# Attention and expert routing on one core: where in the pipeline the load of a pair's values is issued

## The chip, the cores and the metric

The kernel runs on one core of one Trainium2 chip. The time is the device time of one execution in microseconds (us), lower is better. The runs of the kernel before the change took 830.01, 833.48 and 834.38 us, so the median is 833.48 us. Engines are named as in the profile: PE is TensorE's matmul row and PEld its weight loads, DVE is VectorE, ACT is ScalarE, POOL is GpSimd, SP is SyncE, and SPq is SP's sequencer, which here issues DMAs.

## What is computed

Eight batches of eight heads are put through causal attention with a decay bias, and the result goes through a layer of eight experts that takes one expert per token.

```
B, H, S, D = 8, 8, 576, 64
scores = q @ k.T / sqrt(D)
cum = cumsum(max(s, 0), -1)
scores = where(causal, -1e9, scores + min(-(cum_i - cum_j), 0))
attn = softmax(scores)
x = (attn @ v).transpose(0, 2, 1, 3).reshape(B * S, H * D)

logits = x @ w_gate + modality_bias[modality_id]
e = argmax(logits); gate = softmax(logits)[e]
out = gate * (relu(x @ w1[e]) @ w2[e])
```

## The kernel before

**Two halves.** The first, class `Attn`, does the attention in 32 pairs. A pair is one head of two batches, 576 positions each. The second half takes the tokens, sorted by expert, in blocks of 256 rows and multiplies them with w1 and w2. The change touches the first half alone.

**A pair.** Queries and keys come as raw tiles, `rawq` and `rawk`, and are split for float precision into a high part (`QH`, `KA`) and a low part. POOL does the splitting in `prep` (L312 to L342): two copies rawk to KA (L322), two copies rawq to QH (L322), two subtractions into QL and two into KA (L326). Between them SP copies KA's upper rows into another tile, KB (L332), which also gets the rows of the decay bias (L249, L250, in the first pairs L262 and L281). PE multiplies KA with QH (L372) and KB with QL (L394) into a score, DVE adds the mask and finds the row maximum (L396), ACT takes the exponential (L416), PE turns the result over (L433, L448), ACT and DVE copy it to `PT`. Then PE multiplies it with the pair's values, tile `V` (L474): first 20 matmuls for the later queries, and some steps later 8 for the earlier ones. The 20 and the 8 of a pair are the marks by which the text counts pairs. Pair 0 has its 20 at 23.62 us of the profiled execution, pair 1 at 34.85, and pair 31 at 376.59.

**The steps.** `run` (L501) walks through 32 x 9 steps k. A pair has nine steps, one for each of the nine pieces of its score. The transposes run three steps behind the scores, and the products with V some steps behind those, so the 20 matmuls of a pair fall into the first steps of the next pair. During a pair's steps `prep` prepares the queries and keys of the next pair, and loads are written into the program for later pairs: V in the sixth step (L520), for the next pair, and rawq and rawk in the eighth (L522), for the pair after the next.

**What sets the order.** The program is written in that order, and a scheduler decides at build time how each engine's instructions stand, by readiness in its own reckoning and by the order in which they are written. It also sets the semaphores. SP issues its DMAs strictly in that order: one that must wait holds up all behind it. The tiles `V`, `rawq` and `rawk` come from the pool `ld` with two buffers each (L298, L308), so the load of the V of pair p+2 may not start before the 8 matmuls of pair p have read theirs.

Of the kernel before, what the change touches and what calls it, by code (L numbers as in the profile page):

```python
# [38 lines left out]
class Attn:  # L39
# [318 lines left out]
        return after  # L358

    def start(self, pi, x):  # L360
        st = dict(pi=pi, h=pi % 8, x=x, s={}, high={}, PT=self.PT[pi % 2], V=self.V.pop(pi))
        st["mx"] = self.sm.tile([P, 10], F32, name="mx")
        st["sums"] = self.sm.tile([P, 9], F32, name="sums")
        return st
# [136 lines left out]
    def run(self, npair, newx, done, setup):  # L501

        bg = self.bg = []
        seq = [(pi, i) for pi in range(npair) for i in ORDER]
        sts = {}
        prev, prepg, n = [], None, len(seq)
        for k in range(n + LAG + 9):
            if k < n:
                pi, i = seq[k]
                if k % 9 == 0:  # L510
                    sts[pi] = self.start(pi, newx(pi // 8) if pi % 8 == 0 else sts[pi - 1]["x"])
                    prepg = self.prep(pi + 1) if pi + 1 < npair else None
                with self.behind() if pi or not self.pe else self.tc.issue_after(self.pe[-1]):
                    self.score(sts[pi], i)
                if k in setup:
                    with self.newest():
                        more = setup[k]()
                        if more is not None:
                            bg.append([more, False])
                if k % 9 == 5 and 0 < pi < npair - 1:  # L520
                    self.V[pi + 1] = self.load_v(pi + 1)
                if k % 9 == 7 and 0 < pi < npair - 2:  # L522
                    self.raw[pi + 2] = self.load_qk(pi + 2)
                if prepg is not None:
                    next(prepg, 0)
            if prev and next(prev[0][0], 0) == 0:
                _, st, g = prev.pop(0)
                if g == 0 and st["pi"] % 8 == 7:
                    bg.append([done(st["pi"] // 8, st["x"]), False])
            for j in () if k == LAG else (0, 1) if k == LAG + 1 else (k - LAG,) if LAG < k < n + LAG else ():  # L530
                p0, i0 = seq[j]
                with self.behind():
                    self.trans(sts[p0], i0)
                if i0 in (8, ORDER[-1]):
                    g = int(i0 == 8)
                    prev.append((self.tail(sts[p0], g), sts[p0], g))
            if not prev and k >= n + LAG:
                break
            for b in list(bg):
                if k >= b[1] if b[1] > 1 else k % 9 in QUIET or not b[1]:  # L540
                    with self.newest():
                        b[1] = next(b[0], None)
                    if b[1] is None:
                        bg.remove(b)
        assert not prev
        return bg
# [847 lines left out]
```

## Time and profile before

| | us |
|---|---|
| median of three runs | 833.48 |
| fastest, slowest run | 830.01, 834.38 |
| the profiled execution | 832.43 |
| its span in the profile | 830.6 |
| around the span (832.43 - 830.6) | 1.83 |
| attention, to the end of the last product with V | about 381 |
| expert layer | about 449 |

Both halves are bound by PE, which is busy for 98% of the span. A profile row of the timeline gives the start, the duration, the engine, the line of the program, the operation with the tile written and the tiles read, the shape and a count where like instructions follow each other. A bracket at its end is the idle time of the engine ahead of it and what ended it. That releaser is inferred: where the engine named had long been done, it was another, often a DMA.

### The profile page before, as it was taken

To read this page: it belongs to the slowest core of one execution; us is meant where nothing else is said; L and a number is where in the kernel's file an instruction comes from. 1 tells how busy PE (TensorE), PEld (TensorE's weight loads), DVE (VectorE), ACT (ScalarE), POOL (GpSimd) and SP (SyncE) were. 2 spreads that over 40 slices of the span, in tenths; PEclk is the share of its full clock that TensorE was granted. 3 is DMA by queue.
4 is the path that set the end of the run, shared out by engine and by line. 5 is a ranking of instruction groups with operands and counts; after the bars stand their busy time and mean duration, and the time that the engine had idled before them with its cause. 6 is when DMAs were issued, how large, how long until landed. Compare 5 with 4: busy or idle time off the path is not lost. (4 is left out here: it accounts for less than half of the span.)

```text
span 830.6 us, 16652 instructions
## 1 busy us (share of the span) xinstructions
PE 814.3 (98%) x5692; PEld 698.1 (84%) x5692; DVE 539.6 (65%) x1405; ACT 530.5 (64%) x1196; POOL 360.3 (43%) x383
## 2 busy tenths in 40 slices
PE   7989999999999999999999999999999999999996
PEld 6768788788788888888888999998888999988884
DVE  7655676666766677766479865565666655546874
ACT  6867788878888887876365554454455554445663
POOL 8767777998789877993511000000000000000001
PEclk9999999999999999999999999999999999999999
DMA  7574456777567655737598866555556666555970
GB/s 235 157 221 130 159 184 200 226 228 224 153 192 222 218 178 175 243 136 285 200 374 315 312 258 256 206 220 203 209 200 246 257 257 240 207 191 221 373 241 28
DMA packets 68547, 182.29 MB, mean 219 GB/s; under 512 B 7993, under 2 KB 8889, under 8 KB 68334
## 3 DMA queue, kind: packets, MB, share of 16 engines
q1 hardware_dynamic: 62622, 161.17, 57.5%
q0 software_dynamic: 5840, 20.06, 6.2%
q8 instruction: 45, 0.74, 0.4%
q14 instruction: 40, 0.33, 0.1%
HBM read 144.73 MB, written 26.80 MB: 207 GB/s over the span
## 5 line engine op out<-in xcount | busy, mean ns | idle before, releaser
L1075 POOL DMA_INDIRECT out<-ys,oi x36 | 37.0, 1028 | 368.1 <-ACT ys L1074 296.9
L396 DVE CUSTOM_DVE_ANT_0 pe<-sp,mk 128x512 f32<-128x512 f32 (+3 forms) x256 | 122.4, 488 | 106.0 <-PE sp L394 95.1
L416 ACT ACTIVATE pe<-pe,mx 128x512 f32<-128x512 f32 (+3 forms) x256 | 144.3, 565 | 17.8 <-DVE mx L396 15.0
L437 ACT COPY PT<-pt 128x512 f32<-128x512 f32 (+1 forms) x192 | 97.1, 509 | 23.3 <-PE pt L433 23.3
L433 PE MATMUL pt<-ident,pe 128*128 128x128 f32 x640 | 111.2, 280 | 0.3
L372 PE MATMUL sp<-KA,QH 128*128 128x256 f32 (+2 forms) x256 | 102.6, 403 | 5.2 <-POOL KA L326 3.3
L1091 ACT ACTIVATE hT<-hp 128x512 fp32r<-128x512 f32 x72 | 42.8, 595 | 92.5 <-PE hp L1089 91.7
L474 PE MATMUL o<-PT,V 128*64 128x320 f32 (+4 forms) x896 | 101.8, 367 | 0.0
L474 PEld LDWEIGHTS o<-PT,V 128*64 128x64 f32 x896 | 59.1, 137 | 47.7 <-issue 15.8
L1089 PE MATMUL hp<-xT,wcb 128*128 128x256 f32 x648 | 89.6, 282 | 0.0
L1089 PE MATMUL hp<-xT,wca 128*128 128x256 f32 x624 | 87.4, 282 | 0.5 <-ACT xT L1041 0.5
L433 PEld LDWEIGHTS pt<-ident,pe 128*128 128x128 f32 x640 | 76.8, 144 | 12.6 <-issue 5.3
L326 POOL TENSOR_TENSOR KA<-rawk,KA 64x576 fp32r<-64x576 f32 x62 | 86.9, 1418 | 0.2
L394 PE MATMUL sp<-KB,QL 76*128 76x256 f32 (+2 forms) x256 | 85.5, 337 | 1.5 <-DMA QL<-ek 1.5
L326 POOL TENSOR_TENSOR QL<-rawq,QH 64x576 fp32r<-64x576 f32 x62 | 86.6, 1412 | 0.2
L1089 PEld LDWEIGHTS hp<-xT,wcb 128*128 128x128 f32 x648 | 83.1, 188 | 0.6
L1092 DVE SCALAR_TENSOR_TENSOR hT<-hp,hT 128x512 fp32r<-128x512 f32 x72 | 49.5, 687 | 51.6 <-ACT hT L1091 51.6
L1089 PEld LDWEIGHTS hp<-xT,wca 128*128 128x128 f32 x624 | 80.4, 188 | 1.4 <-issue 0.7
L1064 PE MATMUL y<-wcb,hT 128*128 128x512 f32 x336 | 81.2, 398 | 0.0
L1064 PEld LDWEIGHTS y<-wcb,hT 128*128 128x128 f32 x336 | 62.8, 188 | 14.7
L1089 PE MATMUL hp<-xT,wcc 128*128 128x256 f32 x456 | 64.6, 281 | 0.0
L322 POOL TENSOR_SCALAR KA<-rawk 128x576 fp32r<-128x576 f32 x60 | 39.3, 671 | 58.2 <-PE sp L372 25.0
(285 smaller groups left out, 1620.9 us busy)
## 6 DMA issues: line engine op xcount, KB each, us to landing
wrbw<-in_w SPq DMA_DIRECT2D x104, 512.0 KB
wraw<-in_w SPq DMA_DIRECT2D x56, 512.0 KB
rawq<-in_qkv SPq DMA_DIRECT2D x31, 576.0 KB
rawk<-in_qkv SPq DMA_DIRECT2D x31, 576.0 KB
xg<-lists SPq DMA_DIRECT2D x18, 576.0 KB
V<-in_qkv SPq DMA_DIRECT2D x32, 320.0 KB
KB<-KA SPq DMA_DIRECT2D x62, 144.0 KB
lists<-z SPq DMA_DIRECT2D x8, 576.0 KB
```

The source lines that it names most:

```text
L326: self.last = nc.gpsimd.tensor_tensor(o, i, h, ALU.subtract).ins
L372: self.pe.append(self.nc.tensor.matmul(sp[:, :nn], QH[:, q0:q0 + P], self.KA[u][:, ab, :nn], start=True, stop=False).ins)
L394: self.pe.append(nc.tensor.matmul(sp[:, :nn], QL[:EXT, q0:q0 + P], KB[:EXT, ab, :nn], start=False, stop=True).ins)
L396: ins = nc.vector.tensor_tensor_reduce(out=t[:, :n], in0=sp[:, :n], in1=self.mk[:, 512 - n:512], scale=-0.125, scalar=3.0e38, op0=ALU.add, ...
L416: self.act = nc.scalar.activation(t[:, :n], t[:, :n], AF.Exp, bias=m, scale=-1.0, accum_out=st["sums"][:, o:o + 1]).ins
L433: self.pe.append(nc.tensor.transpose(out=pt[:, o:o + P], in_=pe[:, P * j:P * j + P], identity=self.ident).ins)
L437: cp(w[:, :, :, v:v + P], pt[:, :n * (1 + both)].rearrange("p (a j q) -> p a j q", a=1 + both, q=P))
L474: m = nc.tensor.matmul(o[r, f - q0:q1 - q0], V[:, ab, j, :], PT[:, ab, PTS * j + f if j < 4 else PTW - 64:PTS * j + q1 if j < 4 else PTW], ...
L1064: self.last[0] = nc.tensor.matmul(y[u], hT[:, a, f, P * u:P * u + P], W[4 + f // 2][:, c, 512 * (f % 2):512 * (f % 2) + 512], start=f == 0 ...
L1089: nc.tensor.matmul(hp[:, u], W[k][:, a, f:f + P], xT[:, c, k], start=k == 0 and i == 0, stop=k == 3 and i == 2)
L1091: hi = nc.scalar.activation(hs, hp, AF.Relu)
L1092: lo = nc.vector.scalar_tensor_tensor(hT[:, 1, 2 * m:2 * m + 2], hp, 0.0, hs.bitcast(F32), ALU.max, ALU.subtract)
```

## The change

The load of V is written at another step. Before, the sixth step of a pair issued the load for the next pair. Now the third step of a pair issues the load of this same pair. Pairs 0 and 1, whose values are loaded at the start, are as before.

```diff
-        st = dict(pi=pi, ..., V=self.V.pop(pi))
+        st = dict(pi=pi, ..., V=self.V.pop(pi, None))
...
-                if k % 9 == 5 and 0 < pi < npair - 1:
-                    self.V[pi + 1] = self.load_v(pi + 1)
+                if k % 9 == 2 and pi > 1:
+                    sts[pi]["V"] = self.load_v(pi)
```

On PE, DVE and ACT no instruction changes its place. On SP the loads of V move in pairs 2 to 10, at a few places up to pair 16 by one or two rows, and once at the end. On POOL one scatter of the routing (L732) moves behind one subtraction.

The first place is SP in pairs 1 and 2, as one piece of the difference. KB and KA are the key tiles, `mt` small constants of the routing, rawq and rawk the raw tiles of pair 3 above and of pair 4 below.

```order
 L281 DMA QL_103<-ek 2x64 x2
 L332 DMA KB_107<-KA_105 64x576 x2
-L309 DMA V<-in_qkv 128x640
 L304 DMA rawq<-in_qkv 128x1152
 L304 DMA rawk<-in_qkv 128x1152
```

```order
 L332 DMA KB_108<-KA_106 64x576 x2
+L309 DMA V<-in_qkv 128x640
 L638 DMA mt<-in_mid 128x72
 L639 DMA mt<-in_mb 128x16
-L309 DMA V<-in_qkv 128x640
```

In pair 1 a V stood ahead of the raw tiles of pair 3, and none stands there now. In pair 2 a V stands directly behind the KB copies. It is the V of pair 2 now, where before the V of pair 3 stood behind the constants.

The second place is SP in pair 3, and the pairs up to 8 read alike. In brackets are the semaphores that a row waits for: a DMAHW is that of an earlier DMA, Pool and PE are those of the engines. First before the change:

```order
L332 DMA KB_107<-KA_105 64x576 [waits DMAHW5_49,Pool_49]
L332 DMA KB_107<-KA_105 64x576 [waits DMAHW6_49,Pool_49]
L309 DMA V<-in_qkv 128x640 [waits DMAHW7_49,PE_49]
L304 DMA rawq<-in_qkv 128x1152 [waits DMAHW0_49]
L304 DMA rawk<-in_qkv 128x1152 [waits DMAHW1_49]
```

And with the change:

```order
L332 DMA KB_107<-KA_105 64x576 [waits DMAHW4_49,Pool_49]
L332 DMA KB_107<-KA_105 64x576 [waits DMAHW5_49,Pool_49]
L309 DMA V<-in_qkv 128x640 [waits DMAHW6_49]
L304 DMA rawq<-in_qkv 128x1152 [waits DMAHW7_49]
L304 DMA rawk<-in_qkv 128x1152 [waits DMAHW0_49]
```

The rows stand as before, but this V is that of pair 3 and no longer that of pair 4, and it waits for no semaphore of PE: its buffer has been free for a pair.

The third place is SP at the end of the attention, where the load of the V of pair 31 stands between loads of the first weights (`wraw`) of the expert layer.

```order
 L940 DMA wraw<-in_w 128x1024
-L309 DMA V<-in_qkv 128x640
-L940 ISA
-L940 DMA wraw<-in_w 128x1024
+L940 ISA
+L940 DMA wraw<-in_w 128x1024
+L309 DMA V<-in_qkv 128x640
```

V stands behind one more load of weights there. In pairs 11 to 30 the V of the same pair stands at the same place, or one or two rows from it, in both programs, and waits for PE in both.

More of the change, by code (lines that the diff above doesn't have):

```diff
@@ L360, in start @@
     def start(self, pi, x):
-        st = dict(pi=pi, h=pi % 8, x=x, s={}, high={}, PT=self.PT[pi % 2], V=self.V.pop(pi))
+        st = dict(pi=pi, h=pi % 8, x=x, s={}, high={}, PT=self.PT[pi % 2], V=self.V.pop(pi, None))
         st["mx"] = self.sm.tile([P, 10], F32, name="mx")
```

## The prediction

> **What bounds the kernel.** The page's busy times come first:
>
> ```profile
> span 830.6 us, 16652 instructions
> PE 814.3 (98%) x5692; PEld 698.1 (84%) x5692; DVE 539.6 (65%) x1405; ACT 530.5 (64%) x1196; POOL 360.3 (43%) x383
> ```
>
> PE is idle for 830.6 - 814.3 = 16.3 us of the whole span, and the change takes no work from PE. So it can win only where PE waits or runs slowly, and lose only where it makes PE wait. The view by windows and the waits inside one window tell where PE is disturbed (columns: window, length, busy us of PE, PEld, DVE, ACT and POOL with counts, granted clock, DMA share, GB/s):
>
> ```profile
> 50.00:75.00 25.00, 22.65 (x160) 17.51 (x160) 14.45 (x56) 16.76 (x50) 17.69 (x21) 0.93 0.58 194
> 382.00:831.00 449.00, 441.35 (x2825) 396.42 (x2823) 286.92 (x400) 232.09 (x296) 50.48 (x47) 1.00 0.66 241
> ```
>
> ```profile
> PE sp L372 <- POOL KA L326: 2.3, 2, 1.9
> ```
>
> The expert layer has no load of V. From 50 to 75 us PE loses 2.35 us of 25, and nearly all of it (2.3 us in two waits) is for POOL's last preparation step, the subtractions into KA. The granted clock is under 1 there too.
>
> Next I measure each pair's period by its 20 products with V, in the timeline of PE: pairs 1 to 6, then 10, 11 and 12.
>
> ```profile
> 34.85 2.28 PE L474 MATMUL o<-PT,V 128*64 128x320 f32 x20
> 47.17 2.28 PE L474 MATMUL o<-PT,V 128*64 128x320 f32 x20
> 61.70 3.38 PE L474 MATMUL o<-PT,V 128*64 128x320 f32 x20
> 73.97 2.27 PE L474 MATMUL o<-PT,V 128*64 128x320 f32 x20
> 85.58 2.27 PE L474 MATMUL o<-PT,V 128*64 128x320 f32 x20
> 96.73 2.28 PE L474 MATMUL o<-PT,V 128*64 128x320 f32 x20
> ...
> 141.63 2.27 PE L474 MATMUL o<-PT,V 128*64 128x320 f32 x20
> 153.42 2.28 PE L474 MATMUL o<-PT,V 128*64 128x320 f32 x20
> 164.60 2.27 PE L474 MATMUL o<-PT,V 128*64 128x320 f32 x20
> ```
>
> An undisturbed period is 11.15 us (85.58 to 96.73) or 11.18 (153.42 to 164.60), say 11.16. The periods into pairs 2, 3, 4 and 5 are 12.32, 14.53, 12.27 and 11.61, which is 1.16, 3.37, 1.11 and 0.45 too long, and the one into pair 11 is 11.79, 0.63 too long. From 96.73 to 141.63 four pairs take 44.90, 0.26 over, which I leave in place as extra routing work. **What is to be had is 1.16 + 3.37 + 1.11 + 0.45 + 0.63 = 6.72 us.** The largest piece looks so:
>
> ```profile
> 58.94 0.50 PE L372 MATMUL sp<-KA,QH 128*128 128x512 f32 x1 [1.91 <-POOL KA L326]
> 60.31 0.61 PE L372 MATMUL sp<-KA,QH 128*128 128x512 f32 x1 [0.43 <-POOL KA L326]
> ```
>
> ```profile
> 61.00:62.00 1.00, 1.00 (x4) 0.35 (x5) 0.62 (x1) 0.00 (x0) 0.00 (x0) 0.50 0.94 382
> ```
>
> PE waits 1.91 + 0.43 us at the head of pair 4's scores, then the granted clock is 0.50 and the 20 products of pair 3 take 3.38 us where others take 2.28. So a stall costs its length and about 1.1 us of slow clock.
> [...]
>
> **Why POOL is late.** These rows are SP, PE and POOL in pair 1, then in pair 4:
>
> ```profile
> 25.43 1.18 SPq L332 DMA_DIRECT2D KB<-KA  x2
> 29.37 0.87 PE L474 MATMUL o<-PT,V 128*64 128x256 f32 x8
> 30.28 0.33 SPq L309 DMA_DIRECT2D V<-in_qkv  x1
> 31.14 0.42 SPq L304 DMA_DIRECT2D rawk<-in_qkv  x1
> 37.67 1.31 POOL L322 TENSOR_SCALAR KA<-rawk 128x576 fp32r<-128x576 f32 x2 [4.75 <-PE sp L394]
> ...
> 64.21 1.15 SPq L332 DMA_DIRECT2D KB<-KA  x2
> 68.44 0.87 PE L474 MATMUL o<-PT,V 128*64 128x256 f32 x8
> 69.35 0.33 SPq L309 DMA_DIRECT2D V<-in_qkv  x1
> 70.20 0.82 SPq L304 DMA_DIRECT2D rawk<-in_qkv  x1
> 76.12 1.31 POOL L322 TENSOR_SCALAR KA<-rawk 128x576 fp32r<-128x576 f32 x2 [2.96 <-DMA QL<-ek]
> ```
>
> SP is done with the KB copies at 26.61 and 65.36. Then it stands at the load of V, whose buffer PE frees with the 8 products (ending 30.24 and 69.31), and issues V 0.04 us later. The raw tiles queue behind V, and POOL starts 5.1 us after rawk's issue ended in pair 4 (6.1 in pair 1, with large stores behind). POOL's row names other releasers, but the distance to rawk fits every time. Where POOL isn't held by raw tiles, it starts with the first score of the pair, as in pair 29:
>
> ```profile
> 342.25 0.40 PE L372 MATMUL sp<-KA,QH 128*128 128x512 f32 x1
> 342.24 1.32 POOL L322 TENSOR_SCALAR KA<-rawk 128x576 fp32r<-128x576 f32 x2
> ```
>
> That is about 1.5 us before the 20 products, while at 76.12 POOL starts 2.15 us after them (73.97).
>
> **What the change does, part by part.** The number of loads, their bytes and all work on PE, DVE and ACT stay. On SP, in pairs 2 to 10, V is the pair's own, waits for no PE, and the raw tiles behind it are issued 30.28 - 26.61 = 3.7 us (pair 1, where V is also gone from ahead of them: another 0.3) to 69.35 - 65.36 = 4.0 us (pair 4) earlier. I take 4.0.
>
> Pair 3: its preparation moves from 37.67 to about 33.7, its late end goes, 1.16 us. Pair 4, whose preparation is this:
>
> ```profile
> 44.65 1.01 SPq L304 DMA_DIRECT2D rawk<-in_qkv  x1
> 52.20 1.30 POOL L322 TENSOR_SCALAR KA<-rawk 128x576 fp32r<-128x576 f32 x2 [5.99 <-PE sp L407]
> 57.49 2.77 POOL L326 TENSOR_TENSOR KA<-rawk,KA 64x576 fp32r<-64x576 f32 x2
> ```
>
> Here V hardly waited; rawk was late because all of SP had been pushed back in pair 1. With 4.0 us off, the two subtractions end at 54.9 and 56.3 where they ended at 58.9 and 60.3. PE would have come for the first at 58.94 - 1.91 = 57.03, less the 1.16 already won 55.9, and for the second 0.9 us later: no stall, 3.37 us gone, and with the slow clock pair 5's 1.11. Pair 5 is the tightest:
>
> ```profile
> 70.53 1.41 POOL L326 TENSOR_TENSOR KA<-rawk,KA 64x576 fp32r<-64x576 f32 x1
> 73.33 0.48 PE L372 MATMUL sp<-KA,QH 128*128 128x512 f32 x1
> ```
>
> KA is ready at 71.94 for a PE that comes at 73.33, 1.39 us of slack. PE comes 1.16 + 3.37 + 1.11 = 5.64 us earlier, POOL 4.0: a new wait of 5.64 - 4.0 - 1.39 = 0.25 us. From pair 6 on the second saving of 4.0 comes on top, and 0.45 and 0.63 go. **Sum: 6.72 - 0.25 = 6.5 us.** DVE and ACT, at 14.45 and 16.76 us of the 25, have room for it.
>
> Is V now late? Its usual lead is from the end of the KB copies to its 20 products, 65.36 to 73.97: 8.6 us. The tightest is pair 3, whose V follows KB copies delayed by large stores:
>
> ```profile
> 55.54 1.14 SPq L332 DMA_DIRECT2D KB<-KA  x2
> ```
>
> Less 4.0, V is issued at 52.7; the products come at 34.85 + 2 x 11.16 = 57.2, so 4.5 us. The time that a load of V takes alone is in no row. It is bounded by V and both raw tiles, 69.35 to 76.12, 6.8 us, and by zero; nearest is one load of 512 KB against V's 320, in the rows below 367.84 to 371.72, 3.9 us. I take 3.9: no wait. At 6.8 pair 3 alone would wait, 2.3 us, with a slow clock 3.4.
> [...]
>
> At the end V of pair 31 goes behind one more load of weights:
>
> ```profile
> 367.84 0.38 SPq L940 DMA_DIRECT2D wraw<-in_w  x1
> 368.57 0.37 SPq L309 DMA_DIRECT2D V<-in_qkv  x1
> 370.17 0.34 SPq L940 DMA_DIRECT2D wraw<-in_w  x1
> ...
> 371.72 1.05 POOL L963 TENSOR_SCALAR wca<-wraw 128x1024 fp32r<-128x1024 f32 x1 [1.57 <-DMA wraw<-in_w]
> 376.59 2.28 PE L474 MATMUL o<-PT,V 128*64 128x320 f32 x20
> ```
>
> V's issue moves from 368.57 to 370.6, 6.0 us before its use. Taken as 3.9 us it is free; as 6.8 it costs 0.8. I take none. The scatter behind one subtraction comes 1.4 us later and nothing on PE asks for it there. In pairs 11 to 30 V keeps its place behind the same PE wait.
>
> **How the numbers follow.** The profiled execution took 832.43 (span 830.6 and 1.83 around it), 1.05 under the median of 833.48. Less 6.5 this is 825.9 from the one and 827.0 from the other; I predict 826.5. A change by 0.5%, 4.2 us, is about what a measurement of this kernel tells from none.
>
> - Forecast, the stalls go: 826.5, chance 0.62; 824 to 829 by the residue in pair 5 and the runs' own spread.
> - **Half of it.** The raw tiles are earlier, but pair 4's stall stays, because ekd's and eqd's stores around rawk, or constants on POOL, hold the preparation all the same. For it: rawk to POOL took 6.5 us there (45.66 to 52.20), not 5.1. Against: those stores come after rawk in SP's order. 6.5 - 3.4 = 3.1 us remain, 829.8; chance 0.22, a quarter of that beyond 0.5%.
> - **Nothing.** The releasers in POOL's rows are right, POOL waits for PE (L394, L407) and not for rawk, or the scheduler's order makes the change idle. Against: they name another line at each start, none the last reader of that KA. 832.4; chance 0.11.
> - **Slower: V is late in all of pairs 2 to 10.** If a load of V needs more than the 8.6 us, PE waits with its 20 products in nine pairs. At 10.3 us it is 9 x 1.7 = 15.3 us, less 6.5, 841; it turns slower by 0.5% from 8.6 + (6.5 + 4.2) / 9 = 9.8 us. Against: V and two larger tiles together took 6.8. Chance 0.05.
>
> Faster 0.62 + 0.05 = 0.67, less 0.02 for a shallow forecast: 0.65; same 0.30; slower 0.05. The range 823.5 to 831.0 takes in the forecast and its half, 0.84, with a little off at its ends.
>
> **What would show it.** Right: no row of PE waiting for KA in pairs 3 and 4, the 20 products of pair 3 at 2.28 us, periods of 11.2 throughout, pair 12's at about 158 and the granted clock 1.00 from 50 to 75 us; V without a PE wait, the raw tiles directly behind the KB copies, POOL starting some 4 us earlier. Wrong: POOL starting at the old distance from PE's pairs, a DMA wait ahead of the 20 products, or the gain lost again behind 380 us.

## The result and the profile after

The changed kernel took 826.51 us in the median of eight runs, seven of them between 825.16 and 827.06, against 833.37 us for eight runs of the kernel before (830.01 to 835.79). The eighth run took 2291 us, for a reason that its record does not show, and is left out of the ratio. **The ratio is 0.9916, with a 95% interval of 0.9895 to 0.9937**: faster by 0.84%, about 7 us. The profiled execution took 826.59 us.

The page of the changed kernel, its span and PE's busy time:

```profile
span 824.9 us, 16646 instructions
PE 813.0 (99%) x5692; PEld 699.1 (85%) x5692; DVE 540.3 (66%) x1405; ACT 530.5 (64%) x1196; POOL 359.2 (44%) x383
```

PE's idle time fell from 16.3 to 824.9 - 813.0 = 11.9 us. Its 5692 matmuls are the same, and they took 814.3 - 813.0 = 1.3 us less. The view by windows, for the window in which PE was busy for 22.65 of 25 us before:

```profile
50.00:75.00 25.00, 25.00 (x196) 20.59 (x195) 16.60 (x65) 20.00 (x61) 20.87 (x25) 1.00 0.56 176
```

PE is busy without a gap and the granted clock is 1.00. The 20 products of pairs 1 to 5, then of pairs 10 to 12, in the timeline of PE:

```profile
36.12 2.27 PE L474 MATMUL o<-PT,V 128*64 128x320 f32 x20
47.33 2.27 PE L474 MATMUL o<-PT,V 128*64 128x320 f32 x20
58.57 2.27 PE L474 MATMUL o<-PT,V 128*64 128x320 f32 x20
69.72 2.27 PE L474 MATMUL o<-PT,V 128*64 128x320 f32 x20
80.89 2.28 PE L474 MATMUL o<-PT,V 128*64 128x320 f32 x20
...
136.98 2.28 PE L474 MATMUL o<-PT,V 128*64 128x320 f32 x20
148.15 2.27 PE L474 MATMUL o<-PT,V 128*64 128x320 f32 x20
159.31 2.27 PE L474 MATMUL o<-PT,V 128*64 128x320 f32 x20
```

The periods are 11.21, 11.24, 11.15 and 11.17 us where they were 12.32, 14.53, 12.27 and 11.61, and 11.17 into pair 11, where it was 11.79. No 20 products take longer than 2.28. From pair 1 to pair 12 it is 159.31 - 36.12 = 123.19 us and was 164.60 - 34.85 = 129.75: 6.56 us less. The span fell by only 830.6 - 824.9 = 5.7, since pair 0 came at 24.91 and not at 23.62 in this execution. That start varies from trace to trace (23.16 to 25.32 in this study). Up to there both kernels have the same instructions in the same order, and the granted clock of the start differs: it was 0.50 for 3.41 us in the first trace of before and for 10.24 us here. Still, the start came at 23.79 or later in the four traces of kernels in which all nine loads are moved, and at 23.62 or earlier in the other six; whether that is chance is open.

The chain that was held up, in pair 1 and then in pair 4, from SP's and POOL's timelines:

```profile
26.45 1.15 SPq L332 DMA_DIRECT2D KB<-KA  x2
28.28 0.44 SPq L304 DMA_DIRECT2D rawk<-in_qkv  x1
34.29 1.30 POOL L322 TENSOR_SCALAR KA<-rawk 128x576 fp32r<-128x576 f32 x2 [0.83 <-PE sp L372]
...
60.96 1.15 SPq L332 DMA_DIRECT2D KB<-KA  x2
62.16 0.57 SPq L309 DMA_DIRECT2D V<-in_qkv  x1
63.27 0.44 SPq L304 DMA_DIRECT2D rawk<-in_qkv  x1
69.89 1.30 POOL L322 TENSOR_SCALAR KA<-rawk 128x576 fp32r<-128x576 f32 x2
```

In pair 1 rawk leaves 28.28 - 27.60 = 0.7 us after the KB copies, and left 4.5 us after them before (26.61 to 31.14). In pair 4, V follows the KB copies at once (62.11 to 62.16). POOL begins pair 6 at 69.89, 0.17 us after pair 4's 20 products began, and began 2.15 us after that before.

The traces also record each single transfer (packet) of a DMA with its start, end and size, and those of the raw tiles are known by it: 256 transfers of 4608 bytes in each pair. Before the change the last of them ended at 37.13, 51.71, 63.02 and 75.63 us, and POOL began pairs 3 to 6 at 37.67, 52.20, 63.52 and 76.12, each time 0.5 us later. In the second trace of the kernel before it is 0.5 to 0.6 us. So POOL waited for the raw tiles, whatever releaser its rows name.

### The profile page after: what moved, and what is told of

Read it like the earlier page. It is cut to its first block, busy times and chain, and to the rows that moved or that the text cites. A ratio compares the mean times of both kernels' runs of the same rounds, so it can differ in the third digit from the quotient of the medians.

```text
span 824.9 us, 16646 instructions
## 1 busy us (share of the span) xinstructions
PE 813.0 (99%) x5692; PEld 699.1 (85%) x5692; DVE 540.3 (66%) x1405; ACT 530.5 (64%) x1196; POOL 359.2 (44%) x383
## 5 line engine op out<-in xcount | busy, mean ns | idle before, releaser
L1064 PE MATMUL y<-wca,hT 128*128 128x512 f32 x264 | 63.9, 398 | 0.0
```

Of the source, the lines that this page charges most:

```text
L1064: self.last[0] = nc.tensor.matmul(y[u], hT[:, a, f, P * u:P * u + P], W[4 + f // 2][:, c, 512 * (f % 2):512 * (f % 2) + 512], start=f == 0 ...
```

## The experiments

The table reads two rows of each trace, the starts of the 20 products of pairs 1 and 12. An undisturbed kernel needs 123.2 us between them. The last column is the ratio to the kernel before, measured beside it on the same chip.

| kernel | pair 1 | pair 12 | between | ratio, 95% interval |
|---|---|---|---|---|
| before | 34.85 | 164.60 | 129.75 | |
| before, second trace | 34.50 | 165.57 | 131.07 | |
| the change | 36.12 | 159.31 | 123.19 | 0.9916 (0.9895 to 0.9937) |
| the change, second trace | 35.30 | 158.56 | 123.26 | |
| 1: pair 2's V alone | 34.70 | 160.31 | 125.61 | 0.9951 (0.9933 to 0.9970) |
| 2: all but pair 2's V | 34.41 | 161.96 | 127.55 | 0.9958 (0.9944 to 0.9971) |
| 3: raw tiles ahead of V | 35.41 | 159.68 | 124.27 | 0.9939 (0.9916 to 0.9962) |
| 4: the change, one V buffer | 36.55 | 166.75 | 130.20 | 1.0191 (1.0166 to 1.0216) |
| 5: pair 3's V alone | 34.43 | 167.99 | 133.56 | 1.0001 (0.9984 to 1.0018) |
| 6: V in the ninth step | 35.01 | 162.75 | 127.74 | 0.9967 (0.9952 to 0.9982) |

**1. One load alone.** Of the nine loads that change place against the raw tiles, only that of pair 2's V is moved. Against the kernel before:

```diff
-                if k % 9 == 5 and 0 < pi < npair - 1:
-                    self.V[pi + 1] = self.load_v(pi + 1)
+                if k % 9 == 5 and 1 < pi < npair - 1 or k == 20:
+                    (sts[2] if k == 20 else self.V).update({"V" if k == 20 else pi + 1: self.load_v(2 if k == 20 else pi + 1)})
```

> Only the load of pair 2's V is moved (out of pair 1, to the third step of pair 2); all other loads of V stand as before. Theory (SP stood at this one load from 26.61 to 30.28 us, and the push of 4 us ran on through the stores and KB copies into pairs 3, 4 and 5): the losses of pairs 3, 4 and 5 go, 1.16 + 3.37 + 1.11 = 5.6 us, those of pair 6 (0.45) and 11 (0.63) stay: 827.8 us, ratio 0.9932; rawk of pair 3 leaves some 3.5 us earlier, PE never waits for KA in pairs 3 and 4, POOL still starts about 2 us after the 20 products from pair 4 on. Rival (each of the nine moved loads brings its share): 6.9 / 9 = 0.8 us, 832.6 us, ratio 0.999.

It took 829.02 us, against 834.11 for the kernel before: a gain of 5.1 us by the medians, and of 4.1 by the ratio of 0.9951. One load of nine brings more than half of the gain, so even shares are out. SP and POOL in pair 1, then PE at the heads of the scores of pairs 5 and 12:

```profile
27.82 0.43 SPq L304 DMA_DIRECT2D rawk<-in_qkv  x1
34.12 1.31 POOL L322 TENSOR_SCALAR KA<-rawk 128x576 fp32r<-128x576 f32 x2 [0.53 <-DMA rawk<-in_qkv]
...
68.74 0.50 PE L372 MATMUL sp<-KA,QH 128*128 128x512 f32 x1 [0.31 <-POOL KA L326]
...
147.10 0.50 PE L372 MATMUL sp<-KA,QH 128*128 128x512 f32 x1 [0.24 <-POOL KA L326]
```

Pair 3's preparation starts 3.6 us earlier than in the first trace of before (37.67), and the long stall and the slow clock are gone. Short waits for KA remain at the heads of pairs 5 and 12 (the prediction counts them by their periods, into pairs 4 and 11). V still stands at its old place ahead of pair 4's raw tiles, and SP waits there for 1.1 us (40.12 to 41.23), which pushes what comes behind. From pair 1 to 12 it is 2.4 us over the undisturbed 123.2, where 0.45 + 0.63 = 1.1 was expected, so the gain is smaller than the 5.6 us expected.

**2. The complement.** Pair 2's V stays in pair 1, all later ones are moved. Against the changed kernel:

```diff
-                if k % 9 == 2 and pi > 1:
-                    sts[pi]["V"] = self.load_v(pi)
+                if k % 9 == 2 and pi > 2 or k == 14:
+                    (self.V if k == 14 else sts[pi]).update({2 if k == 14 else "V": self.load_v(2 if k == 14 else pi)})
```

> The complement: the load of pair 2's V stays in pair 1, all later ones are moved. Theory: pair 3 loses its 1.16 us as before; pair 4's raw tiles leave some 0.5 us earlier since no V stands ahead of them in pair 2, so its stall shrinks from 1.91 to about 1.2 us and may still bring the slow clock; only pair 6's and 11's losses go for certain. Gain 1.1 to 2.5 us, 831 to 832.3 us, ratio 0.997 to 0.9987. Rival (even shares): 8 / 9 of 6.9, 827.3 us, ratio 0.9926.

It took 829.78 us, ratio 0.9958: a gain of 3.5 us by the ratio (2.4 to 4.7 by its interval; 4.3 by the medians), more than the 1.1 to 2.5 expected and less than even shares would give. SP and POOL in pairs 2 and 3, and PE at the head of pair 3:

```profile
44.25 0.42 SPq L304 DMA_DIRECT2D rawk<-in_qkv  x1
49.79 1.31 POOL L322 TENSOR_SCALAR KA<-rawk 128x576 fp32r<-128x576 f32 x2 [3.39 <-issue]
57.80 0.43 SPq L304 DMA_DIRECT2D rawk<-in_qkv  x1
63.26 1.31 POOL L322 TENSOR_SCALAR KA<-rawk 128x576 fp32r<-128x576 f32 x2 [5.37 <-PE pt L433]
```

```profile
45.08 0.50 PE L372 MATMUL sp<-KA,QH 128*128 128x512 f32 x1 [0.81 <-POOL KA L326]
46.45 0.50 PE L372 MATMUL sp<-KA,QH 128*128 128x512 f32 x1 [0.43 <-POOL KA L326]
47.35 3.97 PE L474 MATMUL o<-PT,V 128*64 128x320 f32 x20
```

Pair 3's stall is back, as expected, and here it brought the slow clock. In pair 2 no V stands ahead of the raw tiles. The issue of rawk ends at 44.67, 1.0 us earlier than before (45.66), but POOL starts 2.4 us earlier (52.20 before): from rawk to POOL it takes 5.1 us instead of 6.5. So the transfer of V counts beside its wait. Its part can be read from the single transfers: with V ahead, the first of the raw tiles came 1.9 us after rawq's issue began (before, 44.17 to 46.06), without it 1.0 us (here, 43.86 to 44.84; 1.0 to 1.1 in the third, fifth and sixth experiments too), so V costs about 0.9 us. The rest is the time that the raw tiles themselves take. In pair 2 it was 5.7 us before, 4.5 here and 7.4 in the fourth experiment, and why it varies is open.

**3. Raw tiles past the wait.** V keeps its step and its wait for PE. The raw tiles, which stood in the eighth step, are written in the fifth and so pass V on SP. Against the kernel before:

```diff
+                if k % 9 == 4 and 0 < pi < npair - 2:
+                    self.raw[pi + 2] = self.load_qk(pi + 2)
                 if k % 9 == 5 and 0 < pi < npair - 1:
                     self.V[pi + 1] = self.load_v(pi + 1)
-                if k % 9 == 7 and 0 < pi < npair - 2:
-                    self.raw[pi + 2] = self.load_qk(pi + 2)
```

> V stays in the preceding pair with its wait for PE, but the raw tiles are written two steps ahead of it, so they pass it on SP. Theory (what counts is that raw tiles no longer queue behind V's wait): the raw tiles leave directly behind the KB copies, POOL starts as with the change, gain 5 to 6.5 us, 827 to 828.5 us, ratio 0.992 to 0.994; something less than the whole since in pair 1 V still holds the stores and KB copies behind it. Rival (what counts is where V's own transfer runs, or POOL waits for PE and not for rawk): no gain, 833.4 us, ratio 1.00.

It took 827.86 us, ratio 0.9939, which is what was expected. SP and POOL in pair 1:

```profile
27.70 0.43 SPq L304 DMA_DIRECT2D rawk<-in_qkv  x1
30.10 0.33 SPq L309 DMA_DIRECT2D V<-in_qkv  x1
33.45 1.31 POOL L322 TENSOR_SCALAR KA<-rawk 128x576 fp32r<-128x576 f32 x2
```

V is issued at 30.10, about as before (30.28), and POOL starts at 33.45 and not at 37.67. This tells the two readings of POOL's rows apart: it waited for the raw tiles, and not for PE. The interval reaches the change's, so whether something is left by V's wait ahead of the stores and KB copies is not settled by the times. The trace has one wait for KA left, 0.56 us at the head of pair 5, and is 1.1 us over the undisturbed 123.2 from pair 1 to 12.

**4. The wait put back.** The change with one V buffer instead of two.

```diff
-        V = self.ld.tile([P, 2, 5, 64], F32, name="V")
+        V = self.ld.tile([P, 2, 5, 64], F32, name="V", bufs=1)
```

> The change, but V has one buffer and not two: each V waits for the 8 products of the pair before its own, which is the moment at which V and the raw tiles behind it left before the change. Theory: in pairs 2 to 8 the raw tiles are held again until the 8 products have ended, rawk of pair 3 too (it stands behind V of pair 1), the stalls of pairs 3 and 4 come back, 831 to 835 us, ratio 0.997 to 1.002. V itself has 4.6 us to its 20 products; if it takes 3.9 us or less nothing is added, if it took 6.8 us PE would wait 2.2 us in each pair, some 900 us. Rival (V's place makes the gain, not the wait): 826.5 us, ratio 0.992.

It took 849.56 us, ratio 1.0191. This was meant to bring back the hold alone and did more. First SP, POOL and PE in pairs 1 to 4, then the end of the attention:

```profile
31.98 0.33 SPq L309 DMA_DIRECT2D V<-in_qkv  x1
32.37 0.42 SPq L304 DMA_DIRECT2D rawk<-in_qkv  x1
54.57 1.31 POOL L322 TENSOR_SCALAR KA<-rawk 128x576 fp32r<-128x576 f32 x2 [9.10 <-DMA eqd<-ek]
61.28 0.80 PE L372 MATMUL sp<-KA,QH 128*128 128x512 f32 x1 [3.64 <-POOL KA L326]
64.22 3.80 PE L474 MATMUL o<-PT,V 128*64 128x320 f32 x20
```

```profile
377.28 0.38 SPq L940 DMA_DIRECT2D wraw<-in_w  x1
377.77 0.36 SPq L309 DMA_DIRECT2D V<-in_qkv  x1
382.01 3.62 PE L474 MATMUL o<-PT,V 128*64 128x320 f32 x20 [6.31 <-DMA V<-in_qkv]
389.90 0.33 SPq L309 DMA_DIRECT2D V<-in_qkv  x1
393.89 2.28 PE L474 MATMUL o<-PT,V 128*64 128x320 f32 x20
```

The hold is back: rawk of pair 3 leaves at 32.37, POOL begins pair 4 at 54.57, and the stall at pair 4's head is longer than before, 3.64 us with the slow clock behind it. From pair 1 to pair 12 it is 130.20 us, as before the change. Pair 3's own 1.16 us did not come back: its raw query tile had left ahead of V, and from rawk to POOL it then took 4.1 us (32.79 to 36.91) and not 6.1. For pair 4 it took 8.3 us (46.30 to 54.57) and not 6.5, which is why that stall is longer than before; what made those transfers slow is open. The rest of the loss is later. There PE waits for V itself: 12.4 us in seven waits over the attention, 6.31 of it in pair 30, whose V stood behind a load of weights that waited for POOL. So this run does not weigh the hold alone. These rows also give V's price: PE went on 4.2 us after V's issue with a load of weights 0.5 us ahead (377.77 to 382.01), and in pair 31, without having waited, 4.0 us after it.

**5. Another single load.** Only the load of pair 3's V is moved. Against the kernel before:

```diff
-                if k % 9 == 5 and 0 < pi < npair - 1:
-                    self.V[pi + 1] = self.load_v(pi + 1)
+                if k % 9 == 5 and 0 < pi < npair - 1 and pi != 2 or k == 29:
+                    (sts[3] if k == 29 else self.V).update({"V" if k == 29 else pi + 1: self.load_v(3 if k == 29 else pi + 1)})
```

> Only the load of pair 3's V is moved, out of pair 2, where it stood directly ahead of pair 4's raw tiles without waiting long for PE. Theory (beside the wait, the 320 KB of V ahead of the raw tiles in the same queues make them land later; without them POOL began pair 4 at 49.79 and not 52.20 us in the second experiment): pair 4's stall of 1.91 us goes or shrinks under 0.5 us, pair 3's 1.16 us stays, and pairs 6 and 11 keep their 0.45 and 0.63: gain 2 to 3.5 us, 830.5 to 832 us, ratio 0.996 to 0.998. Rival (only the wait for PE counts, V's bytes do not): 0.5 us, ratio 0.9995.

It took 834.69 us, ratio 1.0001: no gain, against the theory's 2 to 3.5 us. SP and POOL in pair 3, and PE at the head of pair 5:

```profile
56.05 1.07 SPq L309 DMA_DIRECT2D V<-in_qkv  x2
57.65 0.42 SPq L304 DMA_DIRECT2D rawk<-in_qkv  x1
65.77 1.30 POOL L322 TENSOR_SCALAR KA<-rawk 128x576 fp32r<-128x576 f32 x2 [7.93 <-PE sp L408]
```

```profile
72.48 0.80 PE L372 MATMUL sp<-KA,QH 128*128 128x512 f32 x1 [3.22 <-POOL KA L326]
75.34 4.08 PE L474 MATMUL o<-PT,V 128*64 128x320 f32 x20
```

The stall of pair 4 did go, as the theory had it. But the moved V now stands with pair 4's ahead of pair 5's raw tiles, two V in one place, and rawk to POOL takes 7.7 us (58.07 to 65.77) where it took 5.0 behind one V in the second experiment (58.23 to 63.26). The stall moved from pair 4 to pair 5 and grew. The step that the theory left out is that a load taken from one place is put into another. That the second V alone cost the 2.7 us is not shown. In the single transfers the first of the raw tiles came 2.1 us after rawq's issue began, against 1.7 us in the second experiment. All but the last 10 of the 256 had ended at 63.54, and these 10 followed one after another to 65.29, a tail of 1.75 us that the second experiment does not have. In the first experiment two V also stand ahead of pair 4's raw tiles, 2.6 us apart, and rawk to POOL took 6.1 us there, no longer than behind one. What made the tail is open.

**6. Later still.** The change, with the load in the ninth step.

```diff
-                if k % 9 == 2 and pi > 1:
-                    sts[pi]["V"] = self.load_v(pi)
                 if k % 9 == 7 and 0 < pi < npair - 2:
                     self.raw[pi + 2] = self.load_qk(pi + 2)
+                if k % 9 == 8 and pi > 1:
+                    sts[pi]["V"] = self.load_v(pi)
```

> The change, with the load in the ninth step of the pair and not the third. V then stands behind the raw tiles, and in pair 2 also behind the stores of the decay tables. Theory: pair 2's V is issued about 46.4 us, under 1 us ahead of its 20 products; at the 4.0 to 4.7 us that V alone took at the end of the fourth experiment PE waits about 3.5 us there and then runs on the slow clock for another 1 to 1.7 us; pair 3's V, some 4 us ahead and behind both raw tiles, may cost 1 to 3 us; later pairs keep 6 us or more and wait for nothing. 831 to 834 us, ratio to before 0.997 to 1.001. Rival (V's place is free as long as the raw tiles leave early): 826.5 us, ratio 0.992.

It took 831.23 us, ratio 0.9967, at the lower end of what was expected. V of pair 2 and its 20 products, then V of pair 3 and its 20 products:

```profile
43.98 1.30 SPq L309 DMA_DIRECT2D V<-in_qkv  x1
52.51 0.43 SPq L309 DMA_DIRECT2D V<-in_qkv  x1
```

```profile
49.19 3.88 PE L474 MATMUL o<-PT,V 128*64 128x320 f32 x20 [2.88 <-DMA V<-in_qkv]
62.00 2.27 PE L474 MATMUL o<-PT,V 128*64 128x320 f32 x20
```

Pair 2's V is late by 2.88 us behind the stores, and with the slow clock this costs 4.5 us from pair 1 to pair 12. Pair 3's has 9.5 us, some 4.5 of them through that delay of PE, and waits for nothing, so the 1 to 3 us that it might have cost did not come. So V can be late, in one pair, if it goes another six steps back. With the third step the shortest lead in the change's trace is 6.0 us.

**7 and 8. Both kernels again.** A second trace each.

> The kernel before, for a second trace of it. Theory: the same pairs lose (3, 4, 5, 6 and 11), but the size changes from run to run with the point at which the granted clock falls, since its median of 23 runs is 834.1 and the execution that was profiled took 832.4: losses of 6 to 10 us from pair 1 to pair 12. Rival (the losses are fixed): 6.7 us again.

> The change as it stands, for a second trace. Theory: no pair loses anything, 11.2 us each from pair 1 to 31, whatever the run; only the start up to pair 0's products differs, by up to 1.5 us. Rival: now and then a stall comes back, and the time is 829 us or more.

The kernel before took 833.68 us and lost 131.07 - 123.2 = 7.9 us from pair 1 to 12; in its first trace it was 6.6. The pairs are the same in the main, but the period into pair 5 lost 0.1 us and not 0.45, and the one into pair 8 lost 0.4. PE, at pair 4's head:

```profile
58.46 0.80 PE L372 MATMUL sp<-KA,QH 128*128 128x512 f32 x1 [2.11 <-POOL KA L326]
61.40 4.16 PE L474 MATMUL o<-PT,V 128*64 128x320 f32 x20
```

The wait is like the first trace's, but the 20 products behind it take 4.16 us and not 3.38: the granted clock was 0.50 for 6.83 us here (58.43 to 65.26) and for 3.41 us there (60.56 to 63.97). The change took 825.96 us and again loses nothing (123.26).

## Why the prediction was right, point by point

- **What was to be had.** 6.72 us were read out of the periods, 6.5 of them were forecast, and 6.56 us went between pair 1 and pair 12. Against the medians it is 6.9 us, a little more, since the trace that was read had one of the smaller losses of the kernel before (6.6 against 7.9 in the second). With losses that differ by 1.3 us between two traces, the forecast of 826.5 on a median of 826.51 is as close as that by luck.
- **The mechanism.** Raw tiles stood on SP behind a V that waited for PE. The third experiment takes them past the wait, leaves V in place and gains as forecast. The reading that POOL waited for PE, as its rows say, falls with it, and the single transfers of the raw tiles, with POOL 0.5 us behind the last one, say the same without an experiment.
- **One hold pushes all.** That pair 4's raw tiles were late only because of pair 1 was the right main cause: the first experiment removes pair 1's hold alone and the long stall with it. Pair 4's preparation moved by more than the 4.0 us forecast: it began at 48.04 for a pair 1 at 36.12, so 11.9 us after it, where it began 17.35 after it (52.20, 34.85), 5.4 us earlier. Of that, 5.0 us are rawk's earlier issue: SP's whole row came 4.4 us earlier (the KB copies of pair 2 ended 2.9 us after the start of pair 1's 20 products, where it was 7.3), and V's short wait for PE is gone from ahead of the raw tiles. The last 0.4 us are from rawk to POOL. V's own transfer, which the sum did not have either, still runs ahead of these raw tiles in the change (its last piece ended at 41.95, their first began at 42.10), so at most these 0.4 us can be its. These are pair 4's rows, then KA's last step for pair 5, and between them pair 3's V:

```profile
41.56 0.34 SPq L304 DMA_DIRECT2D rawk<-in_qkv  x1
48.04 1.30 POOL L322 TENSOR_SCALAR KA<-rawk 128x576 fp32r<-128x576 f32 x2 [5.20 <-PE sp L394]
...
52.57 0.58 SPq L309 DMA_DIRECT2D V<-in_qkv  x1
...
67.29 1.43 POOL L326 TENSOR_TENSOR KA<-rawk,KA 64x576 fp32r<-64x576 f32 x1
```

- **The residue of 0.25 us in pair 5** did not come, the period into pair 4 is 11.15 us. Counted from pair 1, KA of pair 5 was ready 4.5 us earlier (71.94 - 34.85 = 37.1 us before, 67.29 + 1.43 - 36.12 = 32.6 now) and not 4.0, and PE came for it 5.5 us earlier, at 69.08, so 0.36 us of the 1.39 us of slack were left. The term was small, and the 4.0 us in it were mis-sized.
- **V's lead.** Pair 3's V has 58.57 - 52.57 = 6.0 us, forecast 4.5; V's own time, taken as 3.9 us from a load of weights, is at most 4.0 in the fourth experiment's pair 31. In the change's trace the last single transfer of pair 3's V ended at 55.42, 2.9 us after its issue began and 3.2 us ahead of its use. The slower rival's mechanism is real, the fourth and sixth experiments show it (PE waited for V for 12.4 us in seven waits and for 2.88 us in one), but not at this step.
- **The end.** V of pair 31, behind one more load of weights, was taken as free with 6.0 us to its use:

```profile
365.24 0.43 SPq L309 DMA_DIRECT2D V<-in_qkv  x1
...
371.26 2.28 PE L474 MATMUL o<-PT,V 128*64 128x320 f32 x20
```

It is 6.0 us, and PE does not wait.
- **The slow clock**, priced at 1.1 us a stall, cost 3.38 - 2.28 = 1.1 there, but 1.3 to 1.9 elsewhere (20 products of 3.62 to 4.16 us). These 20 products show only the part of the slow stretch that falls on them, and the stretch itself was 3.41 us long in some traces and 6.83 in others. This is where the two traces of the kernel before differ most. The forecast did not suffer from it, since its sum was read from whole periods.

## What to carry to other kernels

On an engine that issues in order, as SP did here, an early load whose buffer is not free yet is a wait for all that stands behind it (3.7 us in pair 1 before the change, 26.61 to 30.28); ask not only whether it comes in time but what it holds up. The engine that shows the loss (PE waiting 1.91 us for POOL) can be three steps from the cause (SP waiting for PE), so follow each late start back to the issue of its load, whatever releaser the row names. And when a load is moved, count its bytes out of the old place and into the new one.

## What the runs showed of the hardware that was not expected

Shorter waits than the 1.91 + 0.43 us at pair 4's head before the change were followed by the half clock too, but not in every run. Waits of 0.81 + 0.43 us in the second experiment were followed by 20 products of 3.97 us instead of 2.28; waits of 0.71 + 0.43 at the same place of the fifth were not (2.27). The first of these two in the fifth:

```profile
45.00 0.50 PE L372 MATMUL sp<-KA,QH 128*128 128x512 f32 x1 [0.71 <-POOL KA L326]
```

In the fourth experiment one wait for V was longer than the two waits of the second together, 1.86 against 1.24 us, and the 20 products behind it took 2.27 us all the same:

```profile
341.44 2.27 PE L474 MATMUL o<-PT,V 128*64 128x320 f32 x20 [1.86 <-DMA V<-in_qkv]
```

So the length of a wait alone did not tell in these runs whether the half clock came. The slow stretch had no fixed length either: beside the 3.41 and 6.83 us of the two traces of the kernel before, the granted clock was 0.50 in the fourth experiment from 60.51 to 67.33 and from 377.94 to 384.77 us, 6.8 us each. What decides about the clock is not shown.
